# Four softmax sums of an attention unit completed by one addition and one reciprocal instead of two of each

## The chip, the cores and the metric

The program runs on one core of one Trainium2 chip. The metric is the device time of one execution in microseconds (us); the median of three runs of the kernel before is 2143.24 us (2143.14 to 2144.07).

## What is computed

Attention over 4 batches, 8 heads, 768 tokens and 64 elements a head, in which a token sees the first four tokens (the sinks) and the 128 tokens up to itself; then a mixture of 8 experts over all 3072 tokens, whose gate is balanced over rows and columns in eight rounds. Everything is in 32-bit floats.

```python
keep = is_sink | in_window
scores = np.where(keep, scores, -1000000000.0)
scores = scores - np.max(scores, axis=-1, keepdims=True)
a = np.exp(scores)
a = a / (np.sum(a, axis=-1, keepdims=True) + 1e-09)
out_attn = np.matmul(a, v)
...
for e in range(E):
    out += P[:, e:e + 1] * (np.maximum(x @ w1[e], 0.0) @ w2[e])
```

The change is in the line that divides by the sum plus 1e-9.

## The kernel before, in words

Engines are TensorE (PE, with its weight loads as PEld), VectorE (DVE), ScalarE (ACT), GpSimd (POOL) and SyncE (SP, which issues most transfers).

**Attention** is cut into 48 units: batch, block of 128 tokens, and half of the heads (four heads, in two pairs). A loop over `n` (line 712) takes them in turn and works on several units at once: the scores of unit n+1, the transposed queries and keys of unit n+2, the transposed probabilities of unit n, and the products with the values of unit n-1. The order of the work on PE is the order of the code (`manual_schedule`); the tile framework sets the order of the other engines from the dependences.

One unit runs through the engines like this:

- `transpose_qk` (line 417): PE transposes queries and keys; ACT rounds them to the upper part (L430), DVE forms the rest (L431). Both parts go to the tile `KQ`, from which the scores are formed.
- `scores` (line 444), once for each pair of heads: PE forms 128 x 260 scores a head (L461); DVE masks them and takes the maximum (L464, and a read of its accumulator); ACT takes the exponential in place in the tile `sc`, with the sum as an accumulator (L467, and a read of that accumulator). DVE then adds 1e-9 to the pair's two sums (L468) and takes two reciprocals (L469), both on the small tile `st`; POOL multiplies each head's 128 x 260 exponentials by its reciprocal (L471).
- `transpose_p` (line 473), one pass of the loop later: PE transposes the scaled probabilities (L482); ACT and DVE split them in two parts (L350).
- `split_v` (line 436) on POOL splits the values (L440, L441), and is kept behind the scaling of another unit by `issue_after`. `transpose_sinks` (L496, L497 on POOL, L499 on PE) does the columns of the sinks. `values` (L520) multiplies, and `store_x` (L532, and L540 on ACT and L541 on POOL in the first 16 units) puts the result away. At the start of each batch `split_sinks` adds L403, L406 and L407 on POOL.

Beside the attention PE gets work of the first expert ("fill", L599 and L615); its weights are split on ACT and DVE in `load_plain` (L350 on the tiles `W` and `W2f`), for the first time in four units between 24 and 43 us. After some 300 us come the balancing of the gate and the products of the experts.

The buffers: `sc` and `st` have three copies each, so that three units may be under way; the scores and all transposes share four PSUM banks (`ps_st`).

```python
for h in hs:
    nc.scalar.activation(sc[:, h, :], sc[:, h, :], AF.Exp, bias=nmx[:, h:h + 1], scale=-1.0, accum_out=sm[:, h:h + 1])
```

Of the kernel before, what the change touches and what calls it, by code (L numbers as in the profile page):

```python
# [12 lines left out]
ALU = mybir.AluOpType  # L13
# [216 lines left out]
def tile_sink_attention_moe(ctx: ExitStack, tc: tile.TileContext, q, k, v, wg, w1, w2, out):  # L230

    nc = tc.nc
# [15 lines left out]
    HH = H // 2  # L248
    NP = HH // 2
# [194 lines left out]
    def scores(n, pr):  # L444

        b, i, hh = units[n]
        u = us[n]
        K, Q = KQ[hh][:, :, :, 0:CW], KQ[hh][:, :, :, CW:][:, :, :, turn_of(b, i)]
        if pr == 0:
            u["sc"] = att.tile([P, HH, CW], F32, name="sc", bufs=3)  # L450
            u["st"] = att.tile([P, 3, HH], F32, name="st", bufs=3)
        sc = u["sc"]
        nmx, sm, rs = (u["st"][:, j, :] for j in range(3))
        hs = range(2 * pr, 2 * pr + 2)
        p2 = slice(2 * pr, 2 * pr + 2)
        ps = {h: ps_st.tile([P, CW], F32, name="st") for h in hs}

        for j, (a, c) in enumerate(((0, 0), (0, 1), (1, 0))):
            for h in hs:
                r0 = (h % 2) * D  # L460
                nc.tensor.matmul(ps[h], lhsT=Q[r0:r0 + D, a, pr, :], rhs=K[r0:r0 + D, c, pr, :],  # L461
                                 start=(j == 0), stop=(j == 2))
        for h in hs:
            nc.vector.tensor_tensor_reduce(out=sc[:, h, :], in0=ps[h], in1=masks[place(b, i).start, min(i, 2)], op0=ALU.add, op1=ALU.min,  # L464
                                           scale=-scale, scalar=3.0e38, accum_out=nmx[:, h:h + 1])
        for h in hs:
            nc.scalar.activation(sc[:, h, :], sc[:, h, :], AF.Exp, bias=nmx[:, h:h + 1], scale=-1.0, accum_out=sm[:, h:h + 1])  # L467
        nc.vector.tensor_scalar(rs[:, p2], sm[:, p2], 1e-9, None, op0=ALU.add)  # L468
        nc.vector.reciprocal(rs[:, p2], rs[:, p2])  # L469
        for h in hs:  # L470
            u["scaled"] = nc.gpsimd.tensor_scalar(sc[:, h, :], sc[:, h, :], rs[:, h:h + 1], 1.0, op0=ALU.mult, op1=ALU.mult).ins  # L471

    def transpose_p(n, pr):
# [237 lines left out]
    with tc.manual_schedule(engines={PE}):  # L711
        for n in range(-2, L + 3):
# [15 lines left out]
            if on(n + 1):  # L728
                scores(n + 1, 0)
                scores(n + 1, 1)  # L730
# [336 lines left out]
    hs = {}  # L1067
# [450 lines left out]
```

## Time and profile before

| | before |
|---|---|
| median of 3 runs | 2143.24 us |
| profiled execution, its time | 2143.6 us |
| profiled execution, its span | 2141.9 us |
| PE busy | 2122.1 us (99%) |
| DVE busy | 1539.2 us (72%) |
| ACT busy | 882.2 us (41%) |
| POOL busy | 752.7 us (35%) |
| instructions on DVE | 2821 |

An engine's busy time is the union of its instructions in one profiled execution. A row of the timeline has the start in us, the duration in us, the engine, the line, what is done, written and read, the number of instructions merged into the row, and in brackets the idle time of the engine before it with what ended it. Instructions on one engine overlap at their ends, so what one costs its engine is the step from its start to the next start, which can be less than its duration.

### The profile page before, as it was taken

Reading aid. Unit: us, or ns where it says so; the run is one execution under the profiler, and the core shown is the slowest. Engines: PE = TensorE matmul, PEld = TensorE weight load, DVE = VectorE, ACT = ScalarE, POOL = GpSimd, SP = SyncE. Lnnn points to the kernel's source line nnn. Section 1 sums busy time; section 2 is a strip of 40 time slices with the busy share of each in tenths; the row PEclk is TensorE's granted clock in tenths of the full one; section 3 lists DMA queues with packets and bytes.
Section 4 is the critical chain, followed back from the end, with each engine's and each line's share of the span. In section 5 each row is a group of like instructions: output and inputs, shape, how many; then the busy total and the mean of one; then the engine's idle time right before and its main releaser. Section 6 shows DMA issues by size and latency. Waiting matters only on the chain.

```text
span 2141.9 us, 31828 instructions
## 1 busy us (share of the span) xinstructions
PE 2122.1 (99%) x10501; PEld 1772.8 (83%) x10501; DVE 1539.2 (72%) x2821; ACT 882.2 (41%) x1867; POOL 752.7 (35%) x950
## 2 busy tenths in 40 slices
PE   8999999999999999999999999999999999999998
PEld 7898897888888888888888888888888888888887
DVE  8878878868777777766666666666656666676666
ACT  7777745444444443443332323332333223332222
POOL 7756643333332331132233222232423222232223
PEclk9999999999999999999999999999999999999999
DMA  7434326999999987686666666667866666666662
GB/s 184 95 84 101 85 80 209 328 296 311 296 313 288 317 283 252 226 278 207 198 195 202 203 199 201 201 199 262 301 204 194 201 205 192 202 206 188 206 197 85
DMA packets 397643, 453.83 MB, mean 212 GB/s; under 512 B 99680, under 2 KB 265760, under 8 KB 396576
## 3 DMA queue, kind: packets, MB, share of 16 engines
q1 hardware_dynamic: 397080, 451.57, 67.4%
q8 instruction: 86, 1.41, 0.3%
q14 instruction: 85, 0.70, 0.1%
q10 hardware_dynamic: 392, 0.16, 0.0%
HBM read 314.17 MB, written 137.46 MB: 211 GB/s over the span
## 4 chain that ended last, share of the span: by engine, by line
PE 93%; DVE 3%; ACT 3%; issue 0%; DMA 0%; POOL 0%; SPq 0%; ACTq 0%; DVEq 0%
PE c L784 40%; PE o L1342 20%; PE held L1342 8%; PE held L1028 7%; PE o L1028 7%; PE O L520 3%; PE st L461 2%; PE g L599 1%; PE st L482 1%; ACT sc L467 1%; PE o L615 1%; PE st L426 1%; DVE sc L464 0%; DVE PT L350 0%; ACT PT L350 0%
## 5 line engine op out<-in xcount | busy, mean ns | idle before, releaser
L810 ACT CAST hf<-w 128x512 fp32r<-128x512 f32 x448 | 265.1, 621 | 561.6 <-POOL w L1309 298.8
L1342 PE MATMUL o<-hf,W2q 128*128 128x512 f32 x1920 | 472.1, 390 | 0.0
L1342 PEld LDWEIGHTS o<-hf,W2q 128*128 128x128 f32 x1920 | 360.1, 188 | 75.4 <-DVE acc L1356 0.9
L784 PE MATMUL c<-T,W1q 128*128 128x512 f32 x1530 | 388.9, 390 | 0.2 <-DVE w L1290 0.2
L811 DVE TENSOR_TENSOR hf<-w,hf 128x512 fp32r<-128x512 f32 x448 | 330.6, 766 | 74.6 <-ACT hf L810 67.1
L784 PEld LDWEIGHTS c<-T,W1q 128*128 128x128 f32 x1530 | 286.9, 188 | 60.6 <-DVE w L1290 0.9
L1356 DVE TENSOR_TENSOR acc<-o,acc 128x512 f32<-128x512 f32 x298 | 204.8, 688 | 171.2 <-PE o L1342 171.2
L784 PE MATMUL c<-B,W1q 128*128 128x512 f32 x1134 | 278.3, 390 | 0.0
L1309 POOL TENSOR_TENSOR w<-w 128x512 f32<-128x512 f32 x64 | 82.7, 1292 | 492.5 <-DVE w L1291 492.5
L784 PEld LDWEIGHTS c<-B,W1q 128*128 128x128 f32 x1134 | 212.6, 188 | 43.9
L1290 DVE TENSOR_TENSOR w<-c,M 128x512 f32<-128x512 f32 x192 | 132.4, 690 | 138.3 <-PE c L784 132.1
L1286 ACT COPY M<-c 128x512 f32<-128x512 f32 x192 | 112.8, 588 | 249.9 <-PE c L784 249.8
L1342 PE MATMUL held<-hf,W2q 128*128 128x512 f32 x768 | 194.8, 390 | 0.0
L784 PE MATMUL c<-T,W1f 128*128 128x512 f32 x672 | 171.1, 390 | 1.2 <-DVE C L999 1.0
L1028 PE MATMUL held<-W2f,h 128*128 128x512 f32 x672 | 171.0, 390 | 0.5 <-DVE W2f L811 0.5
L1028 PE MATMUL o<-W2f,h 128*128 128x512 f32 x672 | 170.6, 390 | 0.2 <-DVE acc L1035 0.2
L1342 PEld LDWEIGHTS held<-hf,W2q 128*128 128x128 f32 x768 | 144.1, 188 | 29.8
L1324 POOL TENSOR_TENSOR w<-w 128x512 f32<-128x512 f32 x64 | 105.7, 1651 | 176.1 <-DVE hf L811 176.1
L784 PEld LDWEIGHTS c<-T,W1f 128*128 128x128 f32 x672 | 125.9, 188 | 28.1 <-issue 1.4
L1028 PEld LDWEIGHTS o<-W2f,h 128*128 128x128 f32 x672 | 126.1, 188 | 27.0 <-DVE acc L1035 1.0
L1028 PEld LDWEIGHTS held<-W2f,h 128*128 128x128 f32 x672 | 126.0, 188 | 26.8 <-DVE W2f L811 0.9
L837 POOL TENSOR_TENSOR r<-r 128x256 f32<-128x256 f32 x27 | 20.1, 743 | 358.7 <-ACT M L991 221.2
(216 smaller groups left out, 3105.5 us busy)
## 6 DMA issues: line engine op xcount, KB each, us to landing
W2q<-w2s SPq DMA_DIRECT2D x448, 256.0 KB, 3.2
W1q<-w1s SPq DMA_DIRECT2D x444, 256.0 KB, 2.8
w1s<-W1f SPq DMA_DIRECT2D x56, 896.0 KB, 7.8
w2s<-WT SPq DMA_DIRECT2D x136, 256.0 KB, 3.6
r<-in_moe_w_dram SPq DMA_DIRECT2D x64, 512.0 KB, 3.7
w2s<-W2f SPq DMA_DIRECT2D x56, 256.0 KB, 5.0
PB<-psd SPq DMA_DIRECT2D x16, 512.0 KB, 4.3
w2s<-W2f SPq DMA_DIRECT2D x56, 128.0 KB, 6.6
```

The source lines that it names most:

```text
L461: nc.tensor.matmul(ps[h], lhsT=Q[r0:r0 + D, a, pr, :], rhs=K[r0:r0 + D, c, pr, :], start=(j == 0), stop=(j == 2))
L520: nc.tensor.matmul(u["O"][:, pr], lhsT=x_, rhs=y_, start=(j == 0), stop=(j == len(ops) - 1))
L784: nc.tensor.matmul(ps, lhsT=w1(a, k), rhs=x[:, b, k, :], start=(start and j == 0), stop=(stop and j == len(TERMS) - 1), skip_group_check=n ...
L810: nc.scalar.copy(dst[:, 0], src)
L811: at(1, lambda: nc.vector.tensor_sub(dst[:, 1], src, f32(dst[:, 0])))
L1028: nc.tensor.matmul(o, lhsT=h[c, th][:, a, off:off + P], rhs=W2F[n][:, w, c, :], start=(begin and c == 0 and j == 0), stop=(end and c == 1 ...
L1286: nc.scalar.copy(t, T["c2"])
L1290: nc.vector.tensor_add(w, T["c1"], T[m])
L1309: nc.gpsimd.tensor_sub(S3, T["A11"], T["A21"])
L1324: at(k, lambda: nc.gpsimd.tensor_sub(T["A11"], w, T["A11"]))
L1342: nc.tensor.matmul(o, lhsT=W2Q[part, n, m][:, a, k * P:(k + 1) * P], rhs=F[part, n, H_OF[m]][:, w, :], start=(j == 0 and (begin or not hol ...
L1356: nc.vector.tensor_add(sums[m, k], o, sums[m, k])
```

## The change

`scores` returns after the exponentials of the first pair. Behind the last exponential of the second pair DVE adds 1e-9 to all four sums of the unit in one instruction on 128 x 4 elements and takes four reciprocals in one; then POOL scales all four heads. The numbers that come out are the same.

```diff
@@ -452,7 +452,6 @@
         sc = u["sc"]
         nmx, sm, rs = (u["st"][:, j, :] for j in range(3))
         hs = range(2 * pr, 2 * pr + 2)
-        p2 = slice(2 * pr, 2 * pr + 2)
         ps = {h: ps_st.tile([P, CW], F32, name="st") for h in hs}
@@ -465,9 +464,11 @@
         for h in hs:
             nc.scalar.activation(sc[:, h, :], sc[:, h, :], AF.Exp, bias=nmx[:, h:h + 1], scale=-1.0, accum_out=sm[:, h:h + 1])
-        nc.vector.tensor_scalar(rs[:, p2], sm[:, p2], 1e-9, None, op0=ALU.add)
-        nc.vector.reciprocal(rs[:, p2], rs[:, p2])
-        for h in hs:
+        if pr < NP - 1:
+            return
+        nc.vector.tensor_scalar(rs, sm, 1e-9, None, op0=ALU.add)
+        nc.vector.reciprocal(rs, rs)
+        for h in range(HH):
             u["scaled"] = nc.gpsimd.tensor_scalar(sc[:, h, :], sc[:, h, :], rs[:, h:h + 1], 1.0, op0=ALU.mult, op1=ALU.mult).ins
```

In the program as built DVE has 48 of these additions and 48 reciprocals where it had 96 of each. The orders of PE and of ACT stay as they were. SP swaps one load of the values with a neighbouring load of a weight; POOL keeps its instructions, and in some units the split of the values (L440, L441) now stands in another place beside the sinks' columns (L496, L497). Lines 463 to 467 of the kernel before are one lower in the changed one, L468 and L469 are L469 and L470, and later lines are one higher.

DVE in the first two units, of which the second begins with the fifth masking (L464, in the change L463; the row `ISA st` reads the accumulator). The kernel before, from that fifth masking on:

```order
L464 ISA sc,st<-st,mask_79 128x260
L464 ISA st 128x1
L468 TENSOR_SCALAR st<-st 128x2
L464 ISA sc,st<-st,mask_79 128x260
L464 ISA st 128x1
L469 RECIPROCAL st<-st 128x2
L464 ISA sc,st<-st,mask_79 128x260
L464 ISA st 128x1
L468 TENSOR_SCALAR st<-st 128x2
L464 ISA sc,st<-st,mask_79 128x260
L464 ISA st 128x1
L469 RECIPROCAL st<-st 128x2
```

The change, from the same masking on:

```order
L463 ISA sc,st<-st,mask_79 128x260
L463 ISA st 128x1
L463 ISA sc,st<-st,mask_79 128x260
L463 ISA st 128x1
L463 ISA sc,st<-st,mask_79 128x260
L463 ISA st 128x1
L469 TENSOR_SCALAR st<-st 128x4
L463 ISA sc,st<-st,mask_79 128x260
L463 ISA st 128x1
L470 RECIPROCAL st<-st 128x4
```

The reciprocal of the first unit's first pair stood behind two maskings of the second unit; the one for all four heads stands behind all four of them.

DVE in one of the four units in which it also splits the first expert's weights (L350 on `W2f`). The kernel before:

```order
L350 TENSOR_TENSOR W2f<-r_703,W2f 128x512
L468 TENSOR_SCALAR st<-st 128x2
L350 TENSOR_TENSOR W2f<-r_703,W2f 128x512
L469 RECIPROCAL st<-st 128x2
L468 TENSOR_SCALAR st<-st 128x2
L431 TENSOR_TENSOR KQ_174<-st,KQ_174 128x2x2x128
L469 RECIPROCAL st<-st 128x2
```

The change:

```order
L350 TENSOR_TENSOR W2f<-r_689,W2f 128x512 x2
L469 TENSOR_SCALAR st<-st 128x4
L470 RECIPROCAL st<-st 128x4
L431 TENSOR_TENSOR KQ_174<-st,KQ_174 128x2x2x128
L350 TENSOR_TENSOR PT<-st,PT 128x512 x2
```

Ahead of the queries' and keys' rest (L431) stood an addition, a reciprocal and another addition; now one addition and one reciprocal stand there, and no reciprocal behind it.

## Rows read from the trace of the kernel before

**Rows 1.** Windows: busy time by engine, then granted clock, DMA share and GB/s.

```profile
0.00:30.00 30.00, 23.18 (x121) 18.52 (x122) 25.54 (x97) 19.78 (x58) 23.48 (x65) 0.89 0.81 193
30.00:300.00 270.00, 266.74 (x2235) 239.59 (x2234) 219.67 (x776) 201.50 (x628) 174.10 (x403) 1.00 0.37 90
...
300.00:2141.90 1841.90, 1832.23 (x8151) 1514.66 (x8149) 1293.96 (x1950) 660.89 (x1182) 555.17 (x482) 1.00 0.72 230
```

**Rows 2.** Waits in the attention: us in total, times, longest us.

```profile
DVE st L468 <- ACT sc L467: 21.8, 39, 0.6
...
PEld st L461 <- DVE KQ L431: 6.2, 12, 1.1
```

**Rows 3.** Groups on DVE: busy us, mean ns, then idle before and its releaser.

```profile
L468 DVE TENSOR_SCALAR st<-st 128x2 f32<-128x2 f32 x96 | 23.0, 240 | 25.5 <-ACT sc L467 21.8
L469 DVE RECIPROCAL st<-st 128x2 f32<-128x2 f32 x96 | 15.8, 165 | 2.5
```

**Rows 4.** Timeline of one plain unit, 77 to 85 us.

```profile
77.13 0.74 POOL L541 TENSOR_TENSOR B<-xr,B 128x256 fp32r<-128x256 f32 x1 [0.29 <-ACT B L540]
...
79.09 1.86 POOL L471 TENSOR_SCALAR sc<-sc,st 128x260 f32<-128x260 f32 x4 [1.21 <-ACT sc L467]
79.12 0.56 ACT L430 CAST KQ<-st 128x512 fp32r<-128x512 f32 x1
79.24 0.35 DVE L468 TENSOR_SCALAR st<-st 128x2 f32<-128x2 f32 x1 [0.62 <-ACT sc L467]
...
79.71 0.69 DVE L431 TENSOR_TENSOR KQ<-st,KQ 128x512 fp32r<-128x512 f32 x1
...
84.33 0.47 PEld L482 LDWEIGHTS st<-ident,sc 128*128 128x128 f32 x4
```

**Rows 5.** Timeline of the first unit, 10 to 14 us.

```profile
10.28 0.19 ACT L467 ACTIVATION_READ_ACCUMULATOR sc<-sc,st 128x1 f32 x1
...
10.84 0.40 DVE L464 CUSTOM_DVE_ANT_0 sc<-st,mask 128x260 f32<-128x260 f32 x1
...
11.10 3.85 POOL L471 TENSOR_SCALAR sc<-sc,st 128x260 f32<-128x260 f32 x8 [0.62 <-ACT sc L467]
...
13.17 0.18 PEld L482 LDWEIGHTS st<-ident,sc 128*128 128x128 f32 x1 [0.28 <-POOL sc L471]
```

**Rows 6.** Timeline of the third unit, 16 to 20 us.

```profile
16.38 1.26 DVE L468 TENSOR_SCALAR st<-st 128x2 f32<-128x2 f32 x1
...
16.89 0.71 POOL L441 TENSOR_TENSOR V<-vr,V 128x256 fp32r<-128x256 f32 x1
...
17.42 0.59 ACT L430 CAST KQ<-st 128x512 fp32r<-128x512 f32 x1
...
17.69 1.27 POOL L407 TENSOR_TENSOR VS<-vm,VS 32x512 fp32r<-32x512 f32 x1
17.75 1.23 DVE L468 TENSOR_SCALAR st<-st 128x2 f32<-128x2 f32 x1
...
19.10 0.67 DVE L431 TENSOR_TENSOR KQ<-st,KQ 128x512 fp32r<-128x512 f32 x1
...
19.82 1.07 PEld L461 LDWEIGHTS st<-KQ 64*128 64x128 f32 x11 [1.10 <-DVE KQ L431]
```

**Rows 7.** Timeline of a unit with a weight split, 34 to 37 us.

```profile
34.75 0.74 POOL L541 TENSOR_TENSOR B<-xr,B 128x256 fp32r<-128x256 f32 x1
...
35.03 1.00 DVE L350 TENSOR_TENSOR W2f<-r,W2f 128x512 fp32r<-128x512 f32 x1
...
36.03 0.68 DVE L350 TENSOR_TENSOR W2f<-r,W2f 128x512 fp32r<-128x512 f32 x1
...
36.76 0.68 DVE L431 TENSOR_TENSOR KQ<-st,KQ 128x512 fp32r<-128x512 f32 x1
```

**Rows 8.** Timeline of the first unit of the third batch, 161 to 163 us.

```profile
161.57 0.56 ACT L430 CAST KQ<-st 128x512 fp32r<-128x512 f32 x1
...
162.35 0.67 DVE L431 TENSOR_TENSOR KQ<-st,KQ 128x512 fp32r<-128x512 f32 x1
```

## The prediction

> **What bounds the kernel now.** I read first the busy time by stretch [rows 1]. Behind 300 us PE is busy 1832.2 of 1841.9 us, and nothing that the change touches runs there: that part can only start earlier or later. In the attention the reader is to compare two stretches. From 30 to 300 us PE is busy 266.7 of 270.0 us at a granted clock of 1.00, DVE only 219.7. So PE's idle time there is 3.3 us in all, and 6.8 us in the first 30 us. A change on DVE and POOL that leaves PE's order alone can win little more than what it takes from these waits.
>
> The waits come next [rows 2]. In 39 of the 48 units DVE stands idle, 21.8 us in total, ahead of an addition L468, waiting for ACT's exponentials. That idle time says that DVE had finished the pair-one sums and everything else in its queue and was early. The other row is PE's: its weight loads for the scores waited 12 times, 6.2 us, on L431, the instruction of DVE that stands right behind the sums. That is where a shorter DVE queue could show.
>
> The timeline of a plain unit shows the order of events [rows 4]. The exponentials end shortly ahead of 79.12 us; ACT then rounds the next queries and keys, L430, 79.12 to 79.68; DVE does its second addition and reciprocal inside that time, and L431 starts at 79.71, 0.03 us after L430. I went through all 48 units for the lag of L431 behind L430: in 39 of them it is 0.06 us or less, so ACT sets the time of L431 and not the sums. The exceptions carry the terms below.
>
> **The change, part by part.**
>
> *DVE, removed work.* 48 additions and 48 reciprocals go, half of the two groups: (23.0 + 15.8) / 2 = 19.4 us of DVE time [rows 3]. On 128 x 4 instead of 128 x 2 the remaining ones should cost what they cost now; no row shows that shape, and the bounds are no change and double the mean of 240 and 165 ns, which even so would be +0.4 us a unit on an engine that waits for ACT. I take no change. In the 39 units with idle time ahead of an addition the removed work only makes that idle time longer: worth nothing, and its cover is ACT, whose exponentials and L430 don't change. If that cover were gone, the 19.4 us would come out whole; that is a rival below.
>
> *POOL, moved work.* The scaling L471 now starts behind the second reciprocal. In the plain unit that is 79.24 + 0.35 + 0.165 = 79.76 instead of 79.09 us, 0.7 us later [rows 3, 4]. It waits for all four exponentials, and behind it in POOL's queue stand L440, L441, L496, L497 and, in the first 16 units, L541; all slide by the same 0.7 us, and who waits for them is PE one pass later. The unit's own transposes L482 come at 84.33 us, the scaling ended at 79.09 + 1.86 = 80.95. The slack is 3.4 us and becomes 2.7. I cost this at nothing; cover is PE's own queue of about one pass. The values and the sinks' columns are read by PE later still.
>
> *The first unit* has no such cover. PE's transposes wait for each head's scaling, the last at 13.17 us [rows 5]. Before, scaling could start at 11.10 us, behind the first pair's reciprocal. Now the reciprocal stands behind all four maskings of the second unit in DVE's order. The lower bound is the exponentials: the fourth ended at 10.28 + 0.19 = 10.47, and with 0.17 for each of the two small instructions scaling could start at 10.8, earlier than now, so no loss. The upper bound is DVE's order: its seventh masking started at 10.84, the addition then follows at 11.24, the eighth masking and the reciprocal end some 0.4 and 0.17 later, 11.8 us: +0.7. I take **+0.5 us**, near the end that is read from the order on DVE. Everything behind moves by it.
>
> *The third unit* gives time back. There L468 took 1.26 and 1.23 us where its mean is 0.24 [rows 3], both times beside two-input instructions of POOL: the first ended at 17.64, when L441 had ended at 17.60; the second lay beside L407, 17.69 to 18.96 [rows 6]. L430 ended at 18.01, but L431 waited for both sums and started at 19.10, 1.09 us late, and PE's scores waited 1.10 us for it. With one addition, issued when the exponentials end, there is one meeting with POOL. If it gets in between L441 and L407, as the first one did, the 1.09 us go; if it must outlast L407, nothing goes. I take **-1.1 us**, by the first addition's row.
>
> *Units in which DVE also splits weights* (four, 24 to 43 us). There DVE is busy and the two removed instructions shorten its queue, but L431 still follows ACT within 0.03 to 0.23 us. What moves is POOL's L541: beside it L350 took 1.00 us, without it 0.68 [rows 7]. L541 slides by 0.5 to 0.7 us with the rest of POOL and may meet the second L350, or L431, or nothing. Bounds: 0.32 us better or worse in each of four units, -1.3 to +1.3 us. I take 0.
>
> *Batch starts.* At the third and the fourth batch a long L468 beside L407 holds L431 for 162.35 - 162.13 = 0.22 us behind L430 [rows 8], and 0.23 in the fourth; with one addition 0.19 of it can go in each: **-0.4 us**, between 0 and that.
>
> *The sum* is +0.5 - 1.1 - 0.4 = **-1.0 us**. Against the profiled execution, 2143.6 us (span 2141.9), it gives 2142.6. That execution lies 0.4 us above the median of the runs, 2143.24, so on the median the forecast is **2142.2 us**, no change that a measurement can tell: 0.2%, or 4.3 us, is about what it can tell for this kernel.
>
> A rule speaks against the change. The Trainium skill, Perfetto Trace Analysis, section Optimizing Scalar/DVE Operations, says that grouping helps if the engine is saturated, and that where these engines are not saturated but cause bubbles elsewhere, breaking instructions up lets work finish sooner. By it DVE's idle time would make the merged sums a loss of up to the 0.7 us a unit. The rows show the first half to hold (DVE is not saturated) and the bubble missing, since PE reaches the transposes 3.4 us later.
>
> **The rivals.**
>
> *Later scaling reaches PE (slower).* The rule's case: if the slack of 3.4 us were less than the 0.7 us lost in most units, PE would wait in each: at 0.7 us for 46 units +32 us, about 2175 us. It decides only where POOL's scaling starts 3.4 us later than now. For it: the shift is certain. Against: the factor of five. Chance 0.02.
>
> *POOL's L541 meets the one addition (slower).* In the first 16 units L541 ends at 77.13 + 0.74 = 77.87 us, 1.37 us ahead of the second addition at 79.24 [rows 4]. Slid by 0.7 it ends at 78.6, and 0.7 us remain. If POOL slides by more than 1.4 us, the addition waits out up to 0.74 us of L541 in each of 16 units, L431 with it by about 0.5 us (the sums now lie within L430's 0.56 us), and PE behind that: 16 x 0.5 - 1.0 = +7 us, 2150 us. For it: L468 beside such work did take over 1 us [rows 6]. Against: the remaining 0.7 us, and 0.29 us of POOL's idle time ahead of L541 that absorbs a part. Chance 0.05.
>
> *DVE bounds the attention after all (faster).* If its queue set the pace in most units, up to 19.4 us would go, 2124 us; if it did so only where PE is seen to wait on L431, 6.2 us, 2137 us. For it: DVE is busy 81% of that stretch. Against: the 39 waits for ACT [rows 2]. Chance 0.04.
>
> *The change doesn't do what it says:* excluded, the order as built has 48 of each.
>
> **How the numbers follow.** Forecast 0.89, slower rivals 0.07, faster rival 0.04. The forecast's bounds: low 0 - 1.1 - 0.4 - 1.3 = -2.8 us; high +0.7 + 0 + 0 + 1.3 = +2.0. From 2143.24 that is 2140.4 to 2145.2; with the 0.8 us between the slowest run and the median on the high side and 0.7 us of the 6.2 us on the low side it is 2139.7 to 2146.0. The rivals' 11 in 100 lie outside, and some of the forecast's own, so about 8 in 10 are held. Faster by over 0.2%: 0.04; within: 0.89; slower: 0.07.
>
> **What would show it right or wrong.** Right: behind 300 us PE's busy time is the same; DVE's idle time ahead of L468's successor grows and DVE's busy time falls by some 15 to 25 us (the long additions included); scaling starts 0.6 to 0.9 us later behind the first exponential, in nearly all units; L482 waits on L471 only in the first unit; the first unit's last transpose is some 0.5 us later, the third unit's scores 0.5 us earlier. Wrong: PE loads waiting on L471 in plain units, an addition of over 0.5 us in many units, or a lag of L431 behind L430 that grows.

## The result, and the profile after

The changed kernel takes **2146.72 us** (median of 20 runs, 2145.61 to 2149.0), the kernel before 2143.31 us (20 runs, 2142.64 to 2144.33): ratio 1.0017, interval 1.0011 to 1.0023. It is slower by 3.4 us where -1.0 us was forecast, and 0.7 us above the range. The profiled execution has a span of 2146.8 us against 2141.9.

Windows of the kernel after, as [rows 1]:

```profile
0.00:30.00 30.00, 22.76 (x122) 17.91 (x123) 23.39 (x91) 20.36 (x61) 23.51 (x65) 0.94 0.79 188
30.00:300.00 270.00, 264.62 (x2198) 238.14 (x2196) 204.86 (x682) 200.20 (x621) 173.14 (x404) 0.99 0.37 91
300.00:2146.80 1846.80, 1837.14 (x8186) 1518.57 (x8184) 1298.43 (x1955) 661.98 (x1186) 552.94 (x482) 1.00 0.72 229
```

Behind 300 us PE is idle 9.66 us, before 9.67: that part only starts later. From 30 to 300 us DVE lost 14.8 us of work (219.67 to 204.86), and PE lost too: 2.1 us of busy time, with a granted clock that is no longer 1.00 all through.

Groups on DVE and waits of the kernel after, as [rows 3] and [rows 2]:

```profile
L469 DVE TENSOR_SCALAR st<-st 128x4 f32<-128x4 f32 x48 | 12.1, 252 | 41.5 <-ACT sc L466 41.3
L470 DVE RECIPROCAL st<-st 128x4 f32<-128x4 f32 x48 | 8.5, 178 | 1.5
```

```profile
DVE st L469 <- ACT sc L466: 41.3, 40, 1.3
PEld st L460 <- DVE KQ L431: 9.0, 13, 1.5
...
...
ACT W1f L350 <- POOL r L685: 3.1, 1, 3.1
...
PEld st L483 <- POOL sc L472: 1.7, 4, 0.8
```

On four elements an addition costs 252 ns and a reciprocal 178, nearly as on two, and DVE's idle time ahead of the addition doubled (21.8 to 41.3 us): as forecast, and worth nothing, as forecast. PE's weight loads for the scores now wait 9.0 us on L431 instead of 6.2. The row to stop at is that of W1f: ACT waits for POOL. Before it read 2.5 us.

Where the time goes is read from the time at which PE starts each unit's scores, in one execution of each kernel. The column of before is in us, the others are differences to it (1 to 10 are the experiments below; units are counted from 0):

| unit | before | after | 1 | 2 | 3 | 4 | 7 | 8 | 9 | 10 |
|---|---|---|---|---|---|---|---|---|---|---|
| 4 | 26.63 | -1.23 | -1.13 | -0.21 | -1.03 | -0.81 | -1.18 | -1.05 | -0.86 | -1.01 |
| 15 | 90.73 | -0.27 | -0.12 | +0.03 | -0.02 | +1.28 | -0.21 | +1.08 | +0.24 | +0.04 |
| 16 | 96.50 | +0.64 | +2.04 | +0.02 | +2.13 | +2.15 | -0.18 | +1.06 | +1.15 | +0.96 |
| 27 | 163.06 | +0.68 | +1.34 | +0.01 | +1.38 | +2.19 | -0.19 | +1.04 | +1.14 | +1.01 |
| 28 | 168.25 | +1.32 | +1.99 | +0.02 | +2.01 | +2.83 | -0.34 | +0.90 | +1.77 | +1.67 |
| 39 | 234.84 | +0.91 | +1.57 | +0.04 | +1.62 | +2.41 | -0.75 | +0.50 | +1.36 | +1.25 |
| 40 | 240.05 | +1.52 | +2.20 | +0.04 | +2.23 | +3.05 | -0.93 | +0.33 | +1.98 | +1.89 |
| 41 | 248.02 | +2.22 | +1.74 | -0.38 | +2.92 | +3.06 | -0.23 | -0.11 | +2.67 | +2.60 |
| 42 | 254.70 | +5.29 | +0.98 | -1.03 | +2.92 | +3.03 | +2.89 | -0.89 | +4.15 | +5.63 |
| 47 | 285.79 | +4.89 | +0.46 | -1.60 | +3.02 | +3.07 | +2.48 | -1.38 | +3.79 | +5.27 |

In the column of after, most plain units hold their distance. From unit 15 on it grows in four places: by 0.91, 0.64 and 0.61 us early in the second, third and fourth batch, which begin with units 12, 24 and 36 (units 15 to 16, 27 to 28, 39 to 40), and by 0.70 and 3.07 us from unit 40 to unit 42. Some 0.4 us come back between units 28 and 39, and as much behind unit 42. This execution took 2148.51 us, 1.8 us more than the median of its kernel, so its steps add up to more than the 3.4 us.

**The batch starts.** Timeline of the kernel before, the second batch:

```profile
84.37 1.96 POOL L471 TENSOR_SCALAR sc<-sc,st 128x260 f32<-128x260 f32 x4 [1.04 <-ACT sc L467]
...
89.08 1.27 POOL L407 TENSOR_TENSOR VS<-vm,VS 32x512 fp32r<-32x512 f32 x1
...
90.00 0.39 DVE L468 TENSOR_SCALAR st<-st 128x2 f32<-128x2 f32 x1 [0.62 <-ACT sc L467]
...
90.50 0.67 DVE L431 TENSOR_TENSOR KQ<-st,KQ 128x512 fp32r<-128x512 f32 x1
```

The same place in the kernel after:

```profile
85.14 1.85 POOL L472 TENSOR_SCALAR sc<-sc,st 128x260 f32<-128x260 f32 x4 [1.81 <-DVE st L470]
...
89.63 0.56 ACT L430 CAST KQ<-st 128x512 fp32r<-128x512 f32 x1
89.74 1.27 POOL L407 TENSOR_TENSOR VS<-vm,VS 32x512 fp32r<-32x512 f32 x1
89.75 1.29 DVE L469 TENSOR_SCALAR st<-st 128x4 f32<-128x4 f32 x1 [1.11 <-ACT sc L466]
...
91.17 0.66 DVE L431 TENSOR_TENSOR KQ<-st,KQ 128x512 fp32r<-128x512 f32 x1
...
91.88 0.51 PEld L460 LDWEIGHTS st<-KQ 64*128 64x128 f32 x6 [1.24 <-DVE KQ L431]
```

Unit 13's scaling starts 0.77 us later (85.14 against 84.37; counted from its unit's first exponential it is 1.01 us, since the units are early here), and POOL's queue behind it slides. So L407 starts at 89.74 instead of 89.08, just ahead of unit 14's addition, which ends 0.03 us behind it: 89.75 + 1.29 = 91.04 against 89.74 + 1.27 = 91.01. Before, the addition ended with L407 too, but 0.65 us earlier (90.39). L431 then stands 0.98 us behind the end of L430 (90.19), and PE's weight loads wait 1.24 us. At 162 us, the place of [rows 8], the same: the addition takes 1.17 us, and L431 starts 0.86 us behind L430 where it was 0.22. The Trainium skill, SBUF — State Buffer, section SBUF: two separate sides, says of the ports that DVE and GpSimd share that the instruction that starts first holds them for its whole length and the other fully blocks; of DVE's it counts those in a two-port performance mode and those with two inputs in SBUF. The rows agree: the addition ends with POOL's instruction, whatever its own size. That it is of that kind no run shows by itself.

**Units 40 to 42.** Timeline of the kernel before, 244 to 249 us; `r` on POOL are the sums of the first weight of expert 1 (`sums1`, L682 to L685 before, L683 to L686 after), and W1f is its split on ACT (`first_w1`):

```profile
244.08 0.74 POOL L683 TENSOR_TENSOR r<-r,r 128x256 f32<-128x256 f32 x1
244.16 0.62 ACT L350 CAST W1f<-r 128x512 fp32r<-128x512 f32 x1 [2.46 <-POOL r L684]
244.68 0.51 ACT L467 ACTIVATE sc<-sc,st 128x260 f32<-128x260 f32 x1
...
248.01 0.18 PEld L461 LDWEIGHTS st<-KQ 64*128 64x128 f32 x1 [0.77 <-DVE KQ L431]
```

The kernel after:

```profile
246.29 0.73 POOL L684 TENSOR_TENSOR r<-r,r 128x256 f32<-128x256 f32 x1
246.37 0.62 ACT L350 CAST W1f<-r 128x512 fp32r<-128x512 f32 x1 [3.15 <-POOL r L685]
246.90 0.51 ACT L466 ACTIVATE sc<-sc,st 128x260 f32<-128x260 f32 x1
...
250.23 0.18 PEld L460 LDWEIGHTS st<-KQ 64*128 64x128 f32 x1 [1.52 <-DVE KQ L431]
```

The third piece of W1f stands in ACT's queue ahead of unit 40's exponentials and waits for POOL's sums, which stand behind POOL's scaling. With the scaling late that wait is 3.15 instead of 2.46 us, everything on ACT behind it as much later, and the wait of PE's weight loads 1.52 instead of 0.77 us. That is the 0.70 us. The 3.07 us behind it are the clock. Windows of the kernel after (last three columns: granted clock, DMA share, GB/s):

```profile
246.00:250.00 4.00, 3.15 (x26) 2.67 (x24) 1.55 (x4) 3.63 (x12) 2.62 (x4) 1.00 0.70 160
250.00:254.00 4.00, 3.49 (x19) 2.95 (x20) 3.29 (x12) 3.02 (x11) 3.05 (x9) 0.67 0.01 2
254.00:258.00 4.00, 4.00 (x21) 4.00 (x20) 2.00 (x6) 1.66 (x5) 1.86 (x4) 0.50 0.30 68
```

Behind the wait the granted clock is at its lower level (0.50, 1.2 GHz). At PE's shares this loses 3.49 x 0.33 + 4.0 x 0.50 = 3.2 us. Before, the clock stayed at 1.00 from 246 to 262 us.

### The profile page after: what moved, and what is told of

It reads as the page before. It is cut to its first block, busy times and chain, and to the rows that moved or that the text cites. A ratio compares the mean times of both kernels' runs of the same rounds, so it can differ in the third digit from the quotient of the medians.

```text
span 2146.8 us, 31679 instructions
## 1 busy us (share of the span) xinstructions
PE 2124.5 (99%) x10501; PEld 1774.6 (83%) x10501; DVE 1526.7 (71%) x2725; ACT 882.5 (41%) x1867; POOL 749.6 (35%) x950
## 4 chain that ended last, share of the span: by engine, by line
PE 94%; DVE 3%; ACT 2%; POOL 0%; DMA 0%; issue 0%; SPq 0%; ACTq 0%; DVEq 0%; POOLq 0%
PE c L785 40%; PE o L1343 20%; PE held L1343 8%; PE held L1029 7%; PE o L1029 7%; PE O L521 3%; PE st L460 2%; PE g L600 2%; PE st L483 1%; PE o L616 1%; ACT sc L466 1%; PE st L426 1%; DVE sc L463 0%; PE O L551 0%; DMA w2s<-W2f 0%
```

## Experiments

The theory from these rows: the loss is POOL's lateness, by two ways (L407 beside the addition; W1f ahead of the exponentials), and PE's longer waits let the clock fall. Rivals: the clock falls for another reason; POOL's new order of value and sink splits costs; the single addition itself costs.

**1. The way by W1f taken out of the changed kernel.** `first_w1`:

```diff
-            split(*first_pieces.pop(0))
+            with (tc.issue_after(us[n - 4]["split"][0]) if n >= L - 4 else nullcontext()): split(*first_pieces.pop(0))
```

> The changed kernel with one thing more: the third and fourth piece of the first expert-1 weight (W1f on ScalarE, which read POOL's sums) are held until the probabilities of the unit four before are split, so that they no longer stand ahead of exponentials while POOL's sums are late. POOL's and TensorE's orders stay those of the changed kernel. Theory (POOL's lateness reaches ScalarE through these sums, TensorE then waits 1.5 us, and its clock falls): the wait of W1f on POOL (3.15 us) and the 1.52 us wait of TensorE at 250 us go, the granted clock stays near 1.00 from 250 to 258 us, and the 3.6 us between 241 and 260 us go: 2143.1 us (2142.4 to 2144.0), ratio to before 0.9999. Rival 1 (the clock falls there for another reason and the waits follow from it): clock still near 0.5 at 254 to 258 us and 2146 to 2147 us. Rival 2 (the loss comes from POOL's changed order of value splits and sink splits): no change, 2146.7 us.

Measured: 2143.76 us (2143.09 to 2145.28), ratio 1.0004 (0.9995 to 1.0013). ACT's wait for POOL is gone and so is PE's; column 1 falls from +2.20 to +0.46 where that of after rises to +4.89. Windows:

```profile
250.00:254.00 4.00, 4.00 (x40) 3.86 (x39) 2.82 (x15) 2.89 (x11) 2.20 (x7) 1.00 0.37 78
254.00:258.00 4.00, 4.00 (x35) 3.46 (x35) 3.83 (x8) 3.92 (x10) 3.69 (x9) 1.00 0.22 62
```

Both rivals of this run fall, POOL's order included, since it is that of the changed kernel. Unexpected: the clock fell in another place, from 93 us on, behind the wait at the second batch that is nearly as long in the profile of after (1.20 us here, 1.24 there) without a fall. Column 1 shows it: +2.04 at unit 16, of which all but some 0.5 us is gained back by unit 27 (+1.34, after +0.68).

```profile
90.00:94.00 4.00, 3.00 (x19) 2.09 (x18) 3.90 (x11) 1.96 (x7) 3.92 (x7) 0.92 0.68 161
94.00:98.00 4.00, 4.00 (x25) 3.96 (x25) 2.48 (x9) 3.47 (x12) 3.58 (x10) 0.65 0.50 105
```

**2. The same edit in the kernel before.**

> The kernel before with the same two pieces of W1f held back, and nothing else. Theory: before, W1f waited 2.46 us on POOL's sums and TensorE 0.77 us at 248 us with no fall of the clock, so this gives back 0.5 to 0.8 us: 2142.6 us, ratio 0.9996 to 0.9998. Rival 1 and rival 2: 2143.3 us, ratio 1.0000.

Measured: 2141.76 us (2141.26 to 2142.42), ratio 0.9992 (0.9983 to 1.0002). The gain is about twice the expected one, 1.65 us against 2143.41 for the kernel before, measured beside it: I had counted PE's wait of 0.77 us on L431 alone. In the kernel before a wait of 0.48 us on ACT's L501 follows it, ahead of W1f's fourth piece, and two more of 0.37 and 0.35 us come at unit 43; all are gone here but for the 0.36 us that a plain unit has. So the kernel before already lost time at W1f, and the change made it more.

**3. Pairs again in the units beside L407.** In units 14, 26 and 38 (`pw` stands for the condition on the unit):

```diff
-        if pr < NP - 1:
-            return
-        nc.vector.tensor_scalar(rs, sm, 1e-9, None, op0=ALU.add)
-        nc.vector.reciprocal(rs, rs)
-        for h in range(HH):
+        p2, hs = (slice(2 * pr, 2 * pr + 2), hs) if pw else (slice(0, HH), range(HH))
+        if pr < NP - 1 and len(hs) == HH: return
+        nc.vector.tensor_scalar(rs[:, p2], sm[:, p2], 1e-9, None, op0=ALU.add)
+        nc.vector.reciprocal(rs[:, p2], rs[:, p2])
+        for h in hs:
```

> The changed kernel, but with an addition and a reciprocal for each pair, as before, in three units alone: the first of the second block of the second, third and fourth batch, whose single addition runs beside POOL's subtraction of the sinks' values (L407). POOL's order stays that of the changed kernel. Theory: the steps at 97, 169 and 241 us go (0.9, 0.6 and 0.6 us), the fall of the clock at 250 us stays: 2146.7 - 2.1 = 2144.6 us (2144.2 to 2145.2), ratio 1.0006. Rival 2 (POOL's order): 2146.7 us, ratio 1.0016. Rival 3 (the single addition itself costs everywhere): gain below 0.3 us, 2146.4 us.

Measured: 2146.97 us (2146.17 to 2148.62), ratio 1.0017 (1.0008 to 1.0026): no gain, the steps stay. So it isn't the merging in these units. Timeline of this kernel, and its windows behind 250 us:

```profile
88.98 0.91 DVE L469 TENSOR_SCALAR st<-st 128x2 f32<-128x2 f32 x1
...
89.14 0.73 POOL L441 TENSOR_TENSOR V<-vr,V 128x256 fp32r<-128x256 f32 x1
...
89.95 1.27 POOL L407 TENSOR_TENSOR VS<-vm,VS 32x512 fp32r<-32x512 f32 x1
90.01 1.24 DVE L469 TENSOR_SCALAR st<-st 128x2 f32<-128x2 f32 x1
...
250.94 0.18 PEld L460 LDWEIGHTS st<-KQ 64*128 64x128 f32 x1 [1.51 <-DVE KQ L431]
```

```profile
250.00:254.00 4.00, 2.78 (x23) 2.33 (x24) 3.85 (x14) 3.02 (x10) 3.46 (x9) 1.00 0.13 24
254.00:258.00 4.00, 4.00 (x35) 3.59 (x36) 3.45 (x11) 3.65 (x13) 2.27 (x6) 1.00 0.29 66
```

An addition of two is held as long as one of four, and each pair meets a POOL instruction. What counts is when POOL gets there, and that is set one unit earlier. The other half of the expectation failed in this profile: PE's wait at 250.94 us is as long as in the profile of after, yet the clock stays at 1.00 behind it. It fell at 94 us instead, as in experiment 1.

**4. Pairs again in units 38 to 41.** The edit of experiment 3 with another condition.

> The changed kernel, but with an addition and a reciprocal for each pair, as before, in units 39, 40 and 41 alone (counted from 0; and in unit 38, the first of the fourth batch's second block): the units around the first expert-1 weight. Theory: POOL's sums come 0.7 us earlier against the units, W1f's and TensorE's waits shrink to before's (2.5 and 0.8 us), the clock stays near 1.00 from 250 to 258 us, and the step at 241 us goes too: 2146.7 - 3.6 - 0.6 = 2142.5 us (2142.0 to 2143.8), ratio 0.9996 to 1.0002. Rival 1: the clock still falls, 2146 us. Rival 2: 2146.7 us.

Measured: 2145.78 us (2145.18 to 2146.75), ratio 1.0011 (1.0002 to 1.002). The mechanism came out as expected, the size didn't. W1f waits 2.48 us and PE 0.77 us, before's numbers, the clock stays at 1.00 from 246 to 262 us, and column 4 is flat from unit 40 (+3.05) to unit 47 (+3.07). But the step into unit 40 stays, for the reason that experiment 3 showed; the 3.6 us were read from an execution that lies 1.8 us above its median, so the sum took off too much; and this profile has a fall of the clock at 40 to 44 us (+1.28 at unit 15) that the profile of after hasn't.

**5. Only the scaling late, first attempt.** The kernel before; the four scalings are written behind the second pair's reciprocal, and DVE keeps its pairs.

```diff
-        for h in hs:
+        if pr < NP - 1:
+            return
+        for h in range(HH):
```

> The kernel before with one half of the change alone: VectorE keeps an addition and a reciprocal for each pair, as before, but POOL's four scalings of a unit all wait for the second pair's reciprocal. The order of the instructions on every engine stays that of the kernel before. Theory (POOL's lateness is the whole cost): as the changed kernel, 2146.7 us (2145.6 to 2147.6), ratio 1.0016; TensorE's waits of 1 us or more behind the batch starts at 91 us and near 250 us are there. Rival (the merged addition on VectorE, or POOL's changed order of splits, is what costs): 2143.0 to 2143.8 us.

Measured: 2143.38 us (2142.6 to 2144.19), ratio 1.0001 (0.9992 to 1.001). It doesn't decide what it was made for, since POOL isn't late in it. Timeline (the scaling's lines are two higher here):

```profile
83.96 1.96 POOL L473 TENSOR_SCALAR sc<-sc,st 128x260 f32<-128x260 f32 x4 [1.04 <-ACT sc L467]
...
84.65 0.17 DVE L469 RECIPROCAL st<-st 128x2 f32<-128x2 f32 x1
```

Scaling starts 0.69 us ahead of the second reciprocal: each scaling waits for the columns that it reads, not for its place in the code. Experiment 9 mends this.

**6. What a wait of PE costs.** The kernel of experiment 2, with a delay in six plain units:

```diff
-        nc.vector.tensor_sub(lo, src, f32(hi))
+        for _ in range(4 if n in (18, 20, 22, 30, 32, 34) else 1):
+            nc.vector.tensor_sub(lo, src, f32(hi))
```

> The kernel before with the two pieces of W1f held back (the second experiment) and VectorE's split of the query and key blocks (L431) done four times over in units 18, 20, 22, 30, 32 and 34, with the same values: six delays of 2 us on VectorE in stretches where TensorE waited for nothing. It tells what a wait of TensorE costs. Theory (a wait of 1 us or more can halve the granted clock for some 4 us after it, which costs up to 2 us more): the sum of TensorE's added waits is 5 to 9 us, at least one of the six is followed by a stretch at about 0.5, and the time rises by more than the waits. Rival 1 (the clock falls for another reason): no stretch below 0.9 between 110 and 230 us, and the time rises by the waits alone.

Measured: 2164.38 us (4 runs, 2161.49 to 2165.54), ratio 1.0095 (1.008 to 1.0111). Against experiment 2 that is +22.6 us. The six waits are longer than expected, 14.5 us together. In all PE's waits on that line (L431 there, L432 here) went from 1.7 to 17.0 us, +15.3; the other 7.3 us came behind them. Waits of PE from 100 to 240 us, and windows around the second of the six:

```profile
PE st L462 <- DVE KQ L432: 14.5, 6, 2.6
```

```profile
128.00:130.00 2.00, 0.13 (x2) 0.13 (x4) 1.75 (x4) 0.00 (x0) 0.12 (x1) 1.00 0.00 0
130.00:132.00 2.00, 2.00 (x14) 1.77 (x15) 1.32 (x7) 0.85 (x3) 0.00 (x0) 0.51 0.43 131
132.00:134.00 2.00, 2.00 (x13) 2.00 (x13) 0.83 (x6) 1.24 (x6) 1.15 (x3) 0.63 0.00 0
134.00:136.00 2.00, 2.00 (x21) 2.00 (x20) 0.71 (x2) 1.30 (x3) 1.30 (x5) 1.00 0.10 23
```

Five of the six waits are followed by a stretch at the lower clock (behind 111, 130, 146, 197 and 228 us), the one that ends at 213 us isn't, and nowhere else between 108 and 242 us is the clock below 1.00. So a wait brings the fall about, where there was none before, but not each time; 7.3 us over five falls are about 1.5 us each. These waits are longer than those of the changed kernel; for its 1.5 us there are experiments 1 and 4, in whose profiles that wait is gone or halved and the clock doesn't fall there.

**7. Pairs again in the unit ahead of L407.** The edit of experiment 3 in units 13, 25 and 37.

> The changed kernel, but with an addition and a reciprocal for each pair, as before, in three units alone: the second of the second, third and fourth batch (units 13, 25 and 37), the unit ahead of those of the third experiment; its scaling stands ahead of POOL's work on the sinks' values. Theory, as the third experiment left it (what counts is how late POOL is with L403, L406, L441 and L407, which the unit before sets): L407 starts 0.7 us earlier and the single addition of unit 14 takes under 0.7 us in place of 1.29, and the steps at 97, 169 and 241 us go: 2146.7 - 2.1 = 2144.6 us (2144.0 to 2145.4), ratio 1.0006. If the steps stay: 2146.7 us.

Measured: 2144.43 us (2143.5 to 2145.89), ratio 1.0005 (0.9996 to 1.0014). Timeline of this kernel:

```profile
88.91 1.28 POOL L407 TENSOR_TENSOR VS<-vm,VS 32x512 fp32r<-32x512 f32 x1
...
89.82 0.40 DVE L469 TENSOR_SCALAR st<-st 128x4 f32<-128x4 f32 x1 [1.12 <-ACT sc L466]
...
90.35 0.66 DVE L431 TENSOR_TENSOR KQ<-st,KQ 128x512 fp32r<-128x512 f32 x1
```

The addition of four, where it is still the merged one, now takes 0.40 us and again ends 0.03 us behind L407. All three steps are gone (column 7), and what is left is the way by W1f alone, +0.7 us into unit 41 and +3.1 us into unit 42 in this execution; by the medians it is 1.0 us (2144.43 against 2143.39 for the kernel before).

**8. Both edits together** (1 and 7).

> The first experiment and this call's third together: the changed kernel with W1f's third and fourth piece held back, and pairs in units 13, 25 and 37. Theory: both losses go, and what the change gains at the start (0.2 us) stays: 2143.8 - 2.1 = 2141.7 us (2141.2 to 2142.6), ratio 0.9991, as the kernel before with W1f held back (2141.8 us). Rival (something else of the change costs too): 2143 us or more.

Measured: **2141.18 us** (2140.9 to 2142.12), ratio 0.999 (0.9981 to 0.9999). Both losses are gone, with DVE's sums merged in 45 of 48 units and POOL's order that of the changed kernel. The +1.08 at unit 15 in column 8 is a fall of the clock at 40 to 43 us, as in experiment 4. It beats both kernels; whether it beats experiment 2 (2141.76 us, measured at another time) isn't settled.

**9. Only the scaling late, second attempt.** The kernel before, an addition for each pair, one reciprocal of four:

```diff
-        nc.vector.reciprocal(rs[:, p2], rs[:, p2])
-        for h in hs:
+        if pr < NP - 1: return
+        nc.vector.reciprocal(rs, rs)
+        for h in range(HH):
```

> The kernel before with one half of the change that does make POOL wait: an addition for each pair, as before, and a single reciprocal of all four sums behind the second addition, from which all four scalings read. (The fifth experiment had kept a reciprocal for each pair, and POOL's first scaling still started on the first pair's.) POOL's order is that of the changed kernel but for two rows. Theory (what costs is that POOL's scaling starts 0.7 us later in every unit; how many additions VectorE makes is nothing): 2146.7 us (2145.6 to 2147.6), ratio 1.0016, POOL's scaling at 85.1 us against 84.4 before, the wait of TensorE of 1.2 us at 92 us and of 1.5 us at 250 us. Rival (the single addition of four on VectorE costs): 2143.0 to 2144.0 us.

Measured: 2148.32 us (2146.56 to 2149.22), ratio 1.0023 (1.0014 to 1.0032); the changed kernel, measured beside it, has 2147.86 us. Timeline:

```profile
85.64 1.85 POOL L472 TENSOR_SCALAR sc<-sc,st 128x260 f32<-128x260 f32 x4 [1.81 <-DVE st L470]
...
246.83 0.62 ACT L350 CAST W1f<-r 128x512 fp32r<-128x512 f32 x1 [3.15 <-POOL r L685]
...
250.69 0.18 PEld L461 LDWEIGHTS st<-KQ 64*128 64x128 f32 x1 [1.52 <-DVE KQ L431]
```

The waits are those of the changed kernel to 0.01 us, with two additions on DVE. The whole loss hangs on the moment at which POOL's scaling may start.

**10. The changed kernel once more.**

> The changed kernel as it is, once more, on the chip of the ninth experiment, for a second profile. Theory (a wait of TensorE of 1 to 1.5 us may or may not be followed by a halved clock, which is why its runs lie 3.4 us apart): 2146.7 us, the same four waits at 92, 164, 236 and 250 us, and the stretches at 0.5 behind another choice of them than in the first profile. Rival (the clock falls at 254 us for a reason of that place): the fall again at 250 to 258 us and nowhere else after 30 us.

Measured: 2147.86 us (2145.9 to 2150.26), ratio 1.002 (1.0011 to 1.0029). The waits are the same, and so is the place of the fall (0.71 at 250 to 254 us, 0.50 at 254 to 258): another choice of places didn't come. That the place alone makes it is excluded by experiments 1, 3 and 6, where the clock fell elsewhere, and by 3, where it didn't fall here. Five profiles have the wait of 1.5 us (after, 3, 7, 9 and 10), and in four of them the clock fell behind it; that the longest wait is the likeliest to be followed by a fall fits this, and isn't shown. In experiment 9 the fall behind the same wait cost 1.5 us instead of 3.1 (from unit 41 to 42), so its length differs from run to run, which can make a part of the spread of 3.4 us between the runs of the changed kernel.

## Why the prediction was wrong

- **DVE's removed work** (nothing): right. The two groups fell from 38.8 to 20.6 us, and the time went into idle time ahead of the addition.
- **POOL, moved work** ("I cost this at nothing; cover is PE's own queue"): this is the step that failed. The lateness was forecast as 0.7 us, from one plain unit; counted from each unit's first exponential it is 1.0 us in 31 of the 48 units. That alone would have done nothing, since the slack was 3.4 us. Of its waiters PE was named, and there the cover held: PE's waits on the scaling grew from 1.2 to 1.7 us, in the first unit. Two others weren't named. ACT waits for POOL's sums once, with exponentials queued behind W1f: +0.7 us, and in the profiled execution about 3 us of clock behind it. And DVE's addition, once it has begun beside a two-input instruction of POOL, ended behind it in every profile. Experiments 1 and 9 show the first, 3, 7 and 9 the second.
- **Batch starts** (-0.4): the sign was wrong. The term took L407's place as fixed; it slid with the scaling, and the three starts cost 0.91 + 0.64 + 0.61 = 2.2 us. The rival of L541 described this mechanism to the letter, with the wrong instruction of POOL: L541 held an addition in two units only (0.70 and 0.39 us), L407 in all three starts. The prediction's own sign of being wrong, a growing lag of L431 behind L430, came there: 0.98, 0.86 and 0.85 us, where it had been 0.07, 0.22 and 0.22.
- **First and third unit** (+0.5 and -1.1): the first unit's last transpose is 0.21 us later (13.38 against 13.17 in [rows 5]), within the bounds. The wait of 1.10 us of [rows 6] is gone, and unit 4 starts 1.23 us earlier, though PE waits 1.39 us ahead of it (0.34 us before). All but 0.2 us is lost again by unit 5. DVE is busy 6.26 of the 6.36 us between these two starts, and in them the one addition meets L541 (L542 here), where an addition took 0.15 us before. A gain ahead of a stretch in which DVE is the late one was given back. The rows of after:

```profile
29.48 1.18 POOL L542 TENSOR_TENSOR B<-xr,B 128x256 fp32r<-128x256 f32 x1
29.99 0.70 DVE L469 TENSOR_SCALAR st<-st 128x4 f32<-128x4 f32 x1
```

- **Weight-split and plain units** (0): right but for that one split, the distance to before hardly changes from unit 5 to 15 and from 16 to 27.
- **The clock** was in no term. [rows 1] said 1.00 from 30 to 300 us, and the forecast took that for given; yet 0.89 in the first 30 us, where PE waited, was the hint.
- **The rule** that was weighed, of the Trainium skill, Perfetto Trace Analysis, section Optimizing Scalar/DVE Operations: the rows were said to hold no bubble. They held one, PE's wait of 0.77 us at 248 us, and breaking up did let work finish sooner, by way of ACT and DVE rather than of the transposes.

Settled are the two ways, since with both taken out the change costs nothing (experiment 8 against 2). By the medians the batch starts cost 2.0 us (experiment 1 against 2) and the way by W1f 1.0 us (7 against before), near the 3.4 us measured. Open is what decides whether a given wait is followed by a lower clock.

## What to carry to other kernels

Where a step slides on one engine, list everyone who waits for anything that this engine does behind it, also the rows of the waits view that occur once, and every instruction that shares a resource with it; a slack of 3.4 us to one reader says nothing of the others. When an instruction is long only beside another engine's, look at what sets the other's start before changing its own size: here the cure sat one unit earlier. And merging small instructions on an engine with idle time won nothing here and delayed their first consumer by 1.0 us in most units.

## What the runs showed of the hardware

The same wait of PE was followed by a stretch at the lower clock in some executions and not in others. The wait of its weight loads of 1.5 us at 250 us was followed by one in four of five profiles, that of 1.2 us at 92 us in two of six (experiments 1 and 3), those of its matmuls of 2.2 to 2.6 us in experiment 6 in five of six. Such a stretch cost from 0.5 us (experiment 1) to 3.1 us (after and experiment 7); experiment 6 lost 7.3 us behind 15.3 us of waits. In experiments 4 and 8 the clock fell at 40 us behind waits of 1.2 us at 32 us and 0.9 us at 38 us, which experiments 1 and 3 have without a fall there.

VectorE's additions of 128 x 2 and 128 x 4, 0.17 us when alone, took up to 1.29 us beside POOL's L407 and ended 0.03 us behind it, whenever they had started within it. The subtraction L431, whose one input lies in PSUM, isn't held: in the third unit of the changed kernel it takes its usual 0.69 us in the middle of L407.

```profile
17.89 1.28 POOL L407 TENSOR_TENSOR VS<-vm,VS 32x512 fp32r<-32x512 f32 x1
18.23 0.69 DVE L431 TENSOR_TENSOR KQ<-st,KQ 128x512 fp32r<-128x512 f32 x1 [0.18 <-ACT KQ L430]
```
